# Three turning slots instead of six in the second pass of a channel-attention kernel

## The chip, the cores and the metric

The kernel runs on one core of a Trainium2 chip. The metric is the device time of one execution in microseconds (us). Each kernel is executed several times; the median is given with the lowest and the highest. One more execution is taken under the hardware profiler, and every row of a profile in this document comes from such an execution.

## The reference

The input x has 384 x 384 pixels of 384 channels in bfloat16. The reference takes the mean and the maximum of each channel over all pixels, sends both through the same two small matrices, adds the results, and scales every pixel of x by the sigmoid of the sum:

```python
gap = jnp.mean(xf, 1)
gmp = jnp.amax(xf, 1)
h_a = relu(gap @ w1); h_m = relu(gmp @ w1)     # written with a comparison and a cast
scale = _sigmoid(h_a @ w2 + h_m @ w2)
return x * scale[:, None, None, :]
```

So all of x has to be seen before the first output can be written. The input is 113.25 MB and so is the output. What doesn't fit on the chip between the two passes has to be read a second time.

## The kernel before

**Rows and blocks.** The pixels are counted in rows of 128 pixels, one pixel for each partition; there are 1152 such rows. A block of n rows is one transfer of 128 partitions with n x 768 bytes each; 44 rows are 4224 KB. On the chip there are six slots of 44 rows (`SLOTS`, L17, L118), a buffer `held` of 21 rows, a buffer `acc` of 11 rows for the running maximum, 16 rows kept in PSUM (`kept_ps`) and 2 more in a PSUM bank (`kept_b`).

**First pass (L179 to L207).** SP issues the reads (L184) into the slots in turn. For each block TensorE adds up the channels and VectorE folds the block into `acc` (L200). The last six blocks of 44 rows, the list `stay` (L84), are left in the six slots. `held`, `kept_ps` and `kept_b` hold the first rows of x until the end, and the 11 rows of `acc` are read again when the maximum is done (L228, L235). After that come the small matrices and the sigmoid, whose result stands in `scale_bc` (L241).

**Second pass (L244 to L311).** `put` (L255) multiplies a block by the scale on VectorE, in place (L246), and issues its store from ACT (L264). `get` (L268) reads one of the 20 blocks that are not on the chip, 18 of 44 rows and two of 23 (`AGAIN`, L34), into a slot, issued from SP (L273). The list `order` holds the blocks in the order of their stores. It begins with the six blocks that stayed. After two blocks have been put, the first two slots are read into; after every further block, the slot that has just been put is read into (`read_into`, L281), and the new block is added to the end of `order`. So the six slots turn over in a ring: each read waits until the store of the block six places earlier has landed. The first three blocks are multiplied and stored in small pieces (`FIRST_STORES`, L36), the first read comes in five pieces and the others in one (`FIRST_READS`, L38). When the ring has run out, `held` is multiplied and stored (L304, L305), then the 16 and 2 rows from PSUM, which are multiplied into the slot of the sixth last block, `order[-NS]` (L306 to L311).

**What sets the order.** On SP the instructions of the second pass run in the order in which the program writes them (L292). On the other engines a planner of the framework chooses an order; it may move an instruction forward where it reckons that the engine would otherwise wait. Each engine then runs its own instructions strictly in the planned order, and semaphores set by the framework make an instruction wait for its data or for its buffer.

Of the kernel before, what the change touches and what calls it, by code (L numbers as in the profile page):

```python
# [36 lines left out]

FIRST_READS = ((8, 8, 8, 10, 10), (44,))  # L38
LEAD = 2

ACC_STORES_AT = 3
SUM_TAIL = 4
# [4 lines left out]
def kernel(  # L47
# [15 lines left out]
    NS = len(SLOTS)  # L63
# [5 lines left out]
    def rows_of(ap, first, n):  # L69

        return ap[first * P:(first + n) * P, :].rearrange("(p n) c -> p n c", n=n)
# [12 lines left out]
    stay = []  # L84
# [159 lines left out]
    def multiply(dst, src):  # L244
        n = dst.shape[1]
        nc.vector.tensor_tensor(  # L246
            out=dst, in0=src, in1=scale_bc.unsqueeze(1).to_broadcast([P, n, C]), op=ALU.mult
        )

    def put_acc():  # L250
        for lo, hi in acc_pieces:
            multiply(acc[:, lo:hi, :], acc[:, lo:hi, :])
            nc.scalar.dma_start(out=acc_rows(orr, lo, hi), in_=acc[:, lo:hi, :])

    def put(block, pieces, acc_at=None):  # L255

        first, n, s = block
        j = 0
        for i, m in enumerate(pieces):
            if i == acc_at:  # L260
                put_acc()
            rows = slots[s][:, j:j + m, :]
            multiply(rows, rows)
            nc.scalar.dma_start(out=rows_of(orr, first, n)[:, j:j + m, :], in_=rows)  # L264
            j += m
        assert j == n
# [7 lines left out]
        assert j == 0  # L274


    order = list(stay)
    again.sort(key=lambda b: -b[1])
    stores, reads = list(FIRST_STORES), list(FIRST_READS)

    def read_into(s):  # L281
        fits = [b for b in again if b[1] <= SLOTS[s]]
        if fits:
            b = fits[0]
            again.remove(b)
            b = (*b, s)
            get(b, reads.pop(0) if reads else (b[1],))
            order.append(b)
# [5 lines left out]
    while k < len(order):  # L294
        put(order[k], stores.pop(0) if stores else (order[k][1],), None if k else ACC_STORES_AT)
        k += 1
        if k == LEAD:
            for j in range(k):
                read_into(order[j][2])
        elif k > LEAD:  # L300
            read_into(order[k - 1][2])
    in_order.close()
    assert not again
    multiply(held, held)  # L304
    nc.scalar.dma_start(out=rows_of(orr, held_at, HELD_ROWS), in_=held)  # L305
    s = order[-NS][2]  # L306
    n = PSUM_ROWS + BANK_ROWS
    multiply(slots[s][:, 0:PSUM_ROWS, :], kept_ps)
    nc.scalar.dma_start(out=rows_of(orr, 0, PSUM_ROWS), in_=slots[s][:, 0:PSUM_ROWS, :])
# [30 lines left out]
```

## Time and profile before

| | |
|---|---|
| median of 3 runs | 737.6 us (736.33 to 738.21) |
| profiled execution | 737.92 us |
| its span, first to last instruction | 736.1 us |
| bytes read, written | 196.85 MB, 113.25 MB |
| mean rate over the span | 421 GB/s |
| VectorE busy | 490.2 us, 67% of the span |
| TensorE matmul busy | 128.1 us, 17% of the span |
| 44-row reads of the second pass, issue to landing | 27.7 us median |
| 44-row stores, issue to landing | 79.7 us median |

A line of instructions gives the source line, the engine, the operation, what is written and read, and how often; the numbers behind it are busy time, the mean duration, and the idle time of the engine just before, with what ended it. The two hardware queues are q1 (issued from SP) and q10 (issued from ACT). The first pass ends and the second begins at about 276 us: the first multiply by the scale starts at 275.82. The last read lands at 689.88, and from then on only stores run.

### The profile page before, as it was taken

The numbers are of one execution on the slowest core, as the hardware profiler recorded it, in microseconds if no ns is written. First come the engines' busy times: TensorE is split into PE (matmuls) and PEld (weight loads), VectorE is DVE, ScalarE is ACT, GpSimd is POOL, SyncE is SP. The second block draws the span as 40 slices with busy tenths as digits, with TensorE's granted clock in tenths as the row PEclk, the third lists the DMA queues.
The fourth block names the chain that finished last, engine by engine and source line by source line (L and its number), as shares of the span: only waits on it lengthen the run. The fifth ranks groups of instructions, "written<-read, shape, count | busy, mean of one in ns | idle before, by whom it ended". The sixth has DMA issues, their size and how long they took to land.

```text
span 736.1 us, 2598 instructions
## 1 busy us (share of the span) xinstructions
PE 128.1 (17%) x969; PEld 41.1 (6%) x969; DVE 490.2 (67%) x286; ACT 3.3 (0%) x9; POOL 0.7 (0%) x6
## 2 busy tenths in 40 slices
PE   3334454454544550000000000000000000000000
PEld 0111111111111120000000000000000000000000
DVE  6789999999999989999444464444444444445400
ACT  0000000000000000000000000000000000000000
POOL 0000000000000000000000000000000000000000
PEclk9856667655556555555555555555555555555555
DMA  9999999999999979999999999999999999999998
GB/s 382 438 431 435 423 433 423 431 426 431 423 427 418 417 277 370 415 423 438 425 435 439 432 428 435 437 433 428 435 437 433 428 435 437 433 424 436 436 428 346
DMA packets 18956, 310.26 MB, mean 421 GB/s; under 512 B 2464, under 2 KB 3072, under 8 KB 8320
## 3 DMA queue, kind: packets, MB, share of 16 engines
q1 hardware_dynamic: 12464, 196.86, 63.0%
q10 hardware_dynamic: 6480, 113.25, 36.1%
q8 instruction: 7, 0.11, 0.1%
q14 instruction: 5, 0.04, 0.0%
HBM read 196.85 MB, written 113.25 MB: 421 GB/s over the span
## 4 chain that ended last, share of the span: by engine, by line
another core or an unknown queue 39%; DMA 39%; DVE 13%; DVEq 1%; SPq 1%; issue 1%; PE 0%; ACT 0%; ACTq 0%
DMA x<-in_x_dram 32%; DVE acc L200 10%; DMA out_dram<-x 7%; DVE x L246 2%; DVEq L335 1%; SPq L273 1%; SPq L184 0%; DVE acc L223 0%; DVE acc L246 0%; PE bank_a L240 0%; ACT scale_bc L241 0%; DVE small L234 0%; PE bank_a L233 0%; PE bank_a L238 0%
## 5 line engine op out<-in xcount | busy, mean ns | idle before, releaser
L246 DVE TENSOR_TENSOR x<-x,scale_bc 128x16896 bf16<-128x16896 bf16 (+11 forms) x40 | 224.9, 5665 | 188.6 <-DMA x<-in_x_dram 187.4
L200 DVE TENSOR_TENSOR acc<-acc,x 128x2304 bf16<-128x2304 bf16 (+5 forms) x221 | 241.4, 1167 | 12.6 <-DMA x<-in_x_dram 12.3
L157 PE MATMUL bank_a<-x,small 128*1 128x512 bf16 (+3 forms) x894 | 120.9, 571 | 140.4 <-DMA x<-in_x_dram 140.4
L157 PEld LDWEIGHTS <-small 128*1 128x1 bf16 x912 | 37.1, 110 | 229.2 <-issue 226.5
L193 DVE COPY acc<-x 128x4224 bf16<-128x4224 bf16 x1 | 1.3, 1260 | 5.2 <-DMA x<-in_x_dram 5.2
L200 DVE TENSOR_TENSOR acc<-acc,held 128x2304 bf16<-128x2304 bf16 (+2 forms) x4 | 4.6, 1201 | 0.0
L246 DVE TENSOR_TENSOR held<-held,scale_bc 128x8064 bf16<-128x8064 bf16 x1 | 4.4, 4351 | 0.0
L205 DVE COPY kept_ps<-x 128x3072 uint32<-128x3072 uint32 x1 | 3.4, 3355 | 0.0
L246 DVE TENSOR_TENSOR x<-kept_ps,scale_bc 128x6144 bf16<-128x6144 bf16 x1 | 3.4, 3350 | 0.0
L157 PE MATMUL bank_a<-held,small 128*1 128x512 bf16 (+1 forms) x18 | 2.4, 570 | 3.2 <-DMA held<-in_x_dram 3.2
L223 DVE TENSOR_TENSOR acc<-acc 128x384 bf16<-128x384 bf16 (+2 forms) x4 | 2.6, 658 | 0.1
L246 DVE TENSOR_TENSOR acc<-acc,scale_bc 128x1920 bf16<-128x1920 bf16 (+1 forms) x2 | 2.4, 1252 | 0.0
L168 ACT COPY w_sb<-bank_a 65x128 f32<-65x128 f32 x2 | 0.5, 262 | 265.2 <-PE bank_a L157 264.7
L174 PEld LDWEIGHTS <-x 128*128 128x128 bf16 x39 | 1.3, 109 | 0.0
L113 ACT ACT_TABLE_LOAD x1 | 1.3, 1283 | 0.7 <-PEq L324 0.7
L169 PE MATMUL bank_b<-small,w_sb 65*128 65x3 f32 x4 | 1.2, 365 | 0.4 <-ACT w_sb L168 0.4
L174 PE MATMUL bank_b<-small,x 128*128 128x1 bf16 x39 | 1.2, 165 | 0.0
L169 PE MATMUL bank_b<-small,scale_bc 65*128 65x3 f32 x4 | 1.1, 353 | 0.0
L169 PEld LDWEIGHTS bank_b<-small,w_sb 65*128 65x128 f32 x4 | 1.0, 313 | 0.9 <-ACT w_sb L168 0.9
L169 PEld LDWEIGHTS bank_b<-small,scale_bc 65*128 65x128 f32 x4 | 1.1, 323 | 0.0
L234 DVE TENSOR_REDUCE small<-bank_a 128x2 bf16<-128x256 bf16 x1 | 0.4, 427 | 0.6 <-PE bank_b L233 0.6
L233 PE MATMUL bank_a<-ident_bf,acc 128*128 128x128 bf16 x2 | 0.4, 301 | 1.9 <-DVE acc L223 1.9
(27 smaller groups left out, 7.5 us busy)
## 6 DMA issues: line engine op xcount, KB each, us to landing
out_dram<-x ACTq DMA_DIRECT2D x21, 4224.0 KB, 79.7
x<-in_x_dram SPq DMA_DIRECT2D x20, 4224.0 KB, 27.7
x<-in_x_dram SPq DMA_DIRECT2D x4, 4128.0 KB, 51.6
x<-in_x_dram SPq DMA_DIRECT2D x2, 4032.0 KB, 50.0
x<-in_x_dram SPq DMA_DIRECT2D x2, 3456.0 KB, 44.1
x<-in_x_dram SPq DMA_DIRECT2D x3, 2208.0 KB, 23.0
x<-in_x_dram SPq DMA_DIRECT2D x2, 2784.0 KB, 38.1
x<-in_x_dram SPq DMA_DIRECT2D x2, 2592.0 KB, 35.5
```

The costliest lines, as they stand in the source:

```text
L113: nc.scalar.activation(out=scale_bc[0:1, 0:1], in_=pick[0:1, 0:1], func=ACT.Sigmoid)
L157: nc.tensor.matmul(sum_ps[q * QP:q * QP + 1, 0:g * P], lhsT=ones_bf[:, 0:1], rhs=rows[:, k:k + g, q * P:(q + 1) * P], start=(done + k == 0 ...
L168: nc.scalar.copy(out=s_sb[r % 2], in_=sum_ps[:, r * P:(r + 1) * P])
L169: nc.tensor.matmul(gsum_ps, lhsT=s_sb[r % 2], rhs=pick, start=(r == 0), stop=False)
L174: nc.tensor.matmul(gsum_ps[:, q:q + 1], lhsT=rows[:, k, q * P:(q + 1) * P], rhs=ones_bf, start=False, stop=(last and k == n - 1 and q == C ...
L193: nc.vector.tensor_copy(out=acc, in_=rows[:, 0:A, :])
L200: nc.vector.tensor_tensor(out=acc[:, c:e, :], in0=acc[:, c:e, :], in1=rows[:, j:j + e - c, :], op=ALU.max)
L205: nc.vector.tensor_copy(out=kept_ps.bitcast(U32), in_=rows.bitcast(U32))
L223: nc.vector.tensor_tensor(out=acc[:, 0:h, :], in0=acc[:, 0:h, :], in1=acc[:, n - h:n, :], op=ALU.max)
L246: nc.vector.tensor_tensor(out=dst, in0=src, in1=scale_bc.unsqueeze(1).to_broadcast([P, n, C]), op=ALU.mult)
L273: nc.sync.dma_start(out=slots[s][:, j:j + m, :], in_=rows_of(xr, first, n)[:, j:j + m, :])
L335: with _tile.TileContext(nc) as tc:
```

## The change

Only the first three blocks of `stay` begin the ring. The other three, `resting`, keep their rows in their slots while the ring of three slots takes all 20 reads, and they are put whole, one after the other, when the loop has ended, before `held`. A read now goes into the slot of the block three places earlier. The rows kept in PSUM are multiplied into the slot of the third last block of the ring. The numbers of reads, multiplies, stores and bytes stay the same; the three resting blocks were also before multiplied and stored in one piece each.

```diff
+TURNING = 3
...
-    order = list(stay)
+    order, resting = list(stay[:TURNING]), list(stay[TURNING:])
...
     in_order.close()
     assert not again
+    for block in resting:
+        put(block, (block[1],))
     multiply(held, held)
     nc.scalar.dma_start(out=rows_of(orr, held_at, HELD_ROWS), in_=held)
-    s = order[-NS][2]
+    s = order[-TURNING][2]
```

## The prediction

> **What bounds the kernel now.** I read the page's slices and queues first, then stretches of the second pass, then who waits, then VectorE's order and the landing times. Busy tenths per fortieth of the span (18.4 us), and the two queues (q1 carries the reads that SP issues, q10 the stores that ACT issues):
>
> ```profile
> span 736.1 us, 2598 instructions
> DVE  6789999999999989999444464444444444445400
> DMA  9999999999999979999999999999999999999998
> GB/s 382 438 431 435 423 433 423 431 426 431 423 427 418 417 277 370 415 423 438 425 435 439 432 428 435 437 433 428 435 437 433 428 435 437 433 424 436 436 428 346
> q1 hardware_dynamic: 12464, 196.86, 63.0%
> q10 hardware_dynamic: 6480, 113.25, 36.1%
> ```
>
> The 16 DMA engines are busy 9 tenths or more nearly everywhere and take 99.1% of the span in these two queues; VectorE is below half in the second pass. Transfers bound the kernel, and the change moves no byte more or less. So the question is only whether some stretch of the second pass stops being full. Stretches of that pass (busy us of each engine with its count, granted clock, DMA share, GB/s last):
>
> ```profile
> 276.00:292.00 16.00, 0.00 (x0) 0.00 (x0) 16.00 (x14) 0.00 (x0) 0.00 (x0) 0.50 0.96 381
> 292.00:312.00 20.00, 0.00 (x0) 0.00 (x0) 20.00 (x7) 0.00 (x0) 0.00 (x0) 0.50 1.01 400
> 400.00:420.00 20.00, 0.00 (x0) 0.00 (x0) 8.97 (x2) 0.00 (x0) 0.00 (x0) 0.50 1.00 433
> 690.00:710.00 20.00, 0.00 (x0) 0.00 (x0) 8.45 (x3) 0.00 (x0) 0.00 (x0) 0.50 1.00 433
> 730.00:736.00 6.00, 0.00 (x0) 0.00 (x0) 0.00 (x0) 0.00 (x0) 0.00 (x0) 0.50 0.47 197
> ```
>
> Reads and stores mixed (400 to 420) and stores alone (690 to 710, after the last read landed at 689.88) move the same 433 GB/s at share 1.00. Only the opening, with its small pieces, and the last 6 us are below that. The waits of the second pass, of VectorE and of SP's queue (us in total, times, longest), and the landing times of the 44-row transfers between 360 and 640:
>
> ```profile
> DVE x L246 <- DMA x<-in_x_dram: 187.4, 18, 11.0
> SPq L273 <- DMA out_dram<-x: 376.2, 20, 23.7
> x<-in_x_dram SPq DMA_DIRECT2D x14, 4224.0 KB, 27.7
> out_dram<-x ACTq DMA_DIRECT2D x14, 4224.0 KB, 79.7
> ```
>
> A read waits for the store that empties its slot. A store takes 79.7 us, four times its share of the queue: four stores stand in line. VectorE's order in the middle (start, us, then the idle time before it):
>
> ```profile
> 399.85 8.96 DVE L246 TENSOR_TENSOR x<-x,scale_bc 128x16896 bf16<-128x16896 bf16 x1 [10.98 <-DMA x<-in_x_dram]
> 419.84 8.96 DVE L246 TENSOR_TENSOR x<-x,scale_bc 128x16896 bf16<-128x16896 bf16 x1 [11.03 <-DMA x<-in_x_dram]
> 428.71 4.35 DVE L246 TENSOR_TENSOR held<-held,scale_bc 128x8064 bf16<-128x8064 bf16 x1
> 439.79 8.96 DVE L246 TENSOR_TENSOR x<-x,scale_bc 128x16896 bf16<-128x16896 bf16 x1 [6.73 <-DMA x<-in_x_dram]
> ```
>
> One block (read, multiply, store) every 19.96 us, of which VectorE works 8.96. And the planner moves work: held is multiplied at 428.71, though its line stands behind the loop. Its store is issued at 695.13, in program order.
>
> **The change, part by part.** The same 20 reads, 26 slot multiplies and stores remain. A 44-row block is 4.325 MB: 10.0 us at 433 GB/s alone, 20.0 us at half of that. What changes is order.
>
> *Opening, until 311 us.* The first three blocks keep their pieces, and so do the first two reads. Cost 0: the rows are those above. VectorE ends the third block at 305.7; before, the fourth to sixth followed at once (three times 8.95).
>
> *Without those three stores in line.* Their place in q10 must be taken by stores of read blocks. The first read block lands at 316.18 (the chain of work; the other landings here are from the issues of single stretches), is multiplied by 325.2 and stored from then; the third block's last store (issued 306.99, landing after 28.3 us, so 335.3) still fills q10 meanwhile. The second read lands at 331.5 (issued 311.25, 20.2 us). From 335.4 the third read shares with the first read block's store. In program order q10 never empties: cost 0.
>
> *Steady turning with three slots.* SP's order puts nothing ahead of the next read but its own slot's store. A round of three blocks takes 3 x 19.96 = 59.9 us of DMA time. One slot's own chain is: SP's issue 0.3, first byte at most 1.7 (the shortest transfer of the pass, 96 KB, landed 1.7 after issue), read 20.0, multiply 8.96, store 20.0 = 51.0 us. The 8.9 us left over is time in which a finished block stands in q10 behind its predecessor, so q10 is never empty, and whenever q1 waits for its next read, q10 has both shares. Cost 0. ACT's issue, which in the trace of before waits at 351.69 and 372.27 for a store four earlier to land, has at most three in flight and stops waiting; worth 0, since the line was full anyway. If the 8.9 us were not there, see the short ring below.
>
> *The end.* Three resting multiplies (3 x 8.95) and stores (3 x 10.0) now lie behind the last read block. Let T be the landing that lets the last 23-row read start. That read (2.26 MB) and the store ahead of it (4.325 MB) take 15.2 us; the other 23-row store 5.2, to T+20.4. The last read lands by T+12.1, is multiplied (4.76) by T+16.9 and stored from T+20.4 to T+25.6. The first resting multiply ends at T+25.8 and its bytes flow by T+27.5: a hole of at most 1.9 us, if the planner leaves the program's order. After it VectorE makes a block in 8.95 and q10 needs 10.0, so no further hole. Held and kept pieces follow as before; kept waits for the slot of the third last ring block, long stored. The last 6 us at 197 GB/s end on the same two-row store: 0.
>
> *If the planner moves the resting multiplies forward*, as it did with held, the hole at the end is gone, and one can open where they stand. Nearest rows: all three and held (4.35) straight after the third block would end VectorE's run at 336.8, the first read block's store could start at 345.7, and q10 is empty from 335.3. The third read, issued at 335.4, runs alone until about 347: idle DMA is the first 1.7 us at most, plus 0.3. Put one by one in the gaps of 11.0, they cost 0 (8.95 fits). If their stores move forward too, they fill q10 as before: 0.
>
> *Sum.* Profiled execution: 737.92 for a span of 736.1; it stands 0.3 above the median of 737.6. The change adds 0 + 0 + 0 and between 0 and 2.0 for one hole, at the end or in the middle, not both. Below nothing: a gain is bounded by what is not full. The opening's 276 to 312 and the last 6 us lie 1.9 + 1.5 + 3.3 us above what 433 GB/s would need and are not touched, so I give at most -1. I take +0.6, nearer the low end, since only two of the orders considered open a hole: 737.6 + 0.6 = 738.2.
>
> **A rule that speaks against it.** The row: at share 1.00 and 19.96 us a block there is no recurring gap in the DMA. The Trainium skill, Perfetto Trace Analysis, section Optimization Strategy, says that a gap repeating on the engine that should be saturated can mean too few buffers; halving the turning buffers invites just that. By that rule a repeating hole would appear at each of 20 reads; by the row's spare 8.9 us none does. The skill's DMA: Bandwidth & Descriptors, section Anatomy of one DMA, fits about 2.0 us fixed per transfer (on another issue path than this one); exposed at 20 reads that would be an estimated 40 us, 778. No run here shows it exposed, and the stores in line cover it in my reckoning.
>
> **Rivals.** *The short ring becomes the bound* (slower). Place: SP's read waits at L273. For it: a read took 27.7 us before, and if a store took as long, the chain would be 27.7 + 8.96 + 27.7 + 0.3 = 64.7, 4.8 over 59.9, and with 20/3 rounds +32 us: 770. It decides once read plus store exceed 50.6 us with nothing in line ahead. Against: 7.7 of the 27.7 is standing behind the previous read (issued each 19.96), which a ring of three doesn't have.
>
> *VectorE holds the ring up* (slower). The planner puts 3 x 8.95 + 4.35 = 31.2 us of resting work in one lump before a ring multiply in the steady part. Cover: its 11.0 idle, 8.9 of waiting in line and 10.0 of a read running alone, 29.9; beyond it both queues are dry, 1.3 + 1.7 = 3.0 us: 740.6, more where such a lump stops the ring twice. It decides from a lump of about 30. For it: held was moved. Against: the idle times are 11.0, so lumps may well be split.
>
> *Faster.* Fewer transfers in flight could run nearer to the best slices of the first pass (438 GB/s): 1.2% of some 400 us, -4.6: 733. Against: mixed and lone stores both stand at 433 with share 1.00.
>
> *No change in effect*: stores and multiplies are both moved forward and the order is nearly that of before; 737.6, inside my forecast.
>
> **How the numbers follow.** A measurement of this kernel can tell about 0.3%, 2.2 us (735.4 to 739.8). Forecast, full throughout with at most one hole, "no change in effect" included: 0.64. VectorE lump: 0.15 (739.9 to 745). Short ring: 0.12 (741 to 770). Faster: 0.09 (731 to 735.3). The range leaves out the upper two thirds of the short ring (0.08) and most of the faster case (0.07): 735.0 to 745.0. Same 0.64, slower 0.27, faster 0.09.
>
> **What would show it.** Right: stretches of 20 us between 340 and 660 at 432 or more; 44-row stores landing in 25 to 40 us instead of 79.7; reads near 20 to 23; VectorE still idle some 11 before each ring multiply; the last read landing some 52 us before the end (25.6 - 12.1 + 30 + held and kept 8.9) where it was 45. Wrong: share below 0.98 in the steady stretches (short ring), a single dip beside a row of resting multiplies (lump), a rate above 436 (faster). The forecast fails if a lone queue with one transfer in flight cannot fill 16 engines: before had deeper lines wherever one queue was alone.

## The result and the profile after

| | median us | lowest to highest | runs |
|---|---|---|---|
| before | 737.05 | 736.33 to 738.21 | 5 |
| after | 740.95 | 740.37 to 742.09 | 5 |

The ratio is 1.0051, with a 95% interval of 1.0036 to 1.0065. The kernel became 3.9 us slower, half a percent. The time lies inside the stated range, but the likeliest case, full throughout with at most one hole and no change to be told (735.4 to 739.8), is not what happened. On another chip the change was measured once more at 1.0036 (1.0023 to 1.0049).

The page of the changed kernel, the lines that answer to those of before:

```profile
span 739.3 us, 2595 instructions
DVE  6789999999999989959564441444444444444440
DMA  9999999999999979999999999999999999999988
GB/s 380 436 431 433 423 431 435 432 426 428 420 428 420 414 265 371 423 427 441 433 411 430 439 439 432 424 433 437 439 435 426 430 435 439 437 426 429 413 353 383
q1 hardware_dynamic: 12464, 196.86, 62.7%
q10 hardware_dynamic: 6480, 113.25, 36.1%
```

Bytes and packets are those of before. The low slices stand at the very end: 413, 353 and 383, where before had 436, 428 and 346. (The 411 in the 21st slice holds the stretch from 375 to 380, at 385 GB/s, but there the two queues' packets together still take 62.8% and 37.7% of the engines' time; in the second profile of the same kernel that stretch is at 433, so it is no mark of the change.) Stretches of the second pass, the steady part first (us of each engine, clock, DMA share, GB/s last):

```profile
400.00:420.00 20.00, 0.00 (x0) 0.00 (x0) 8.98 (x2) 0.00 (x0) 0.00 (x0) 0.50 1.00 433
560.00:580.00 20.00, 0.00 (x0) 0.00 (x0) 9.00 (x2) 0.00 (x0) 0.00 (x0) 0.50 1.00 433
680.00:690.00 10.00, 0.00 (x0) 0.00 (x0) 8.19 (x1) 0.00 (x0) 0.00 (x0) 0.50 0.96 408
690.00:700.00 10.00, 0.00 (x0) 0.00 (x0) 4.76 (x1) 0.00 (x0) 0.00 (x0) 0.50 1.06 434
700.00:710.00 10.00, 0.00 (x0) 0.00 (x0) 2.20 (x1) 0.00 (x0) 0.00 (x0) 0.50 0.95 391
710.00:720.00 10.00, 0.00 (x0) 0.00 (x0) 6.29 (x3) 0.00 (x0) 0.00 (x0) 0.50 0.69 293
```

The steady part is as full with three slots as it was with six: 433 GB/s at share 1.00. From 680 on there is a small dip and then a hole. Against 433 the four last stretches lack 25, -1, 42 and 140 GB/s for 10 us each, 4.8 us of transfer in all; before, the same four stretches (446, 433, 433, 410) lacked 0.2. The last landing is only 3.1 us later in these two executions (738.27 against 735.15), so about 1.5 us of that sum may be coarse counting rather than loss: a packet is counted at its start. Summed by the durations of the packets in the trace, the 16 engines stand idle for 0.4 us in all between 688 and 689.5 and for 2.8 us between 710.5 and 713.5 (in the second profile of the change 0.9 and 3.6 us); before, no stretch between 312 and 730 shows such an idle time. The heart of the hole:

```profile
710.50:713.50 3.00, 0.00 (x0) 0.00 (x0) 3.00 (x2) 0.00 (x0) 0.00 (x0) 0.50 0.18 77
```

Who issues what around the hole:

```profile
688.22 25.20 ACTq L265 DMA_DIRECT2D out_dram<-x  x4
688.75 0.33 SPq L274 DMA_DIRECT2D x<-in_x_dram  x1
690.77 4.76 DVE L247 TENSOR_TENSOR x<-x,scale_bc 128x8832 bf16<-128x8832 bf16 x1 [2.58 <-DMA x<-in_x_dram]
707.80 4.76 DVE L247 TENSOR_TENSOR x<-x,scale_bc 128x8832 bf16<-128x8832 bf16 x1 [12.28 <-DMA x<-in_x_dram]
712.47 3.35 DVE L247 TENSOR_TENSOR x<-kept_ps,scale_bc 128x6144 bf16<-128x6144 bf16 x1
713.45 0.95 ACTq L308 DMA_DIRECT2D out_dram<-held  x1
```

The last read is issued at 688.75 and lands at 707.7. VectorE needs until 712.5, and only then does ACT issue the last ring block's store (712.59), and behind it at once the stores of a resting block (712.97) and of held (713.45). The store ahead had moved its last bytes by 712 and landed at 712.25; the first bytes of the new stores move at 713.4. In between nothing is under way, although held and the resting block had been multiplied long before:

```profile
333.82 17.83 DVE L247 TENSOR_TENSOR x<-x,scale_bc 128x16896 bf16<-128x16896 bf16 x2 [8.42 <-DMA x<-in_x_dram]
359.94 17.83 DVE L247 TENSOR_TENSOR x<-x,scale_bc 128x16896 bf16<-128x16896 bf16 x2 [8.29 <-DMA x<-in_x_dram]
377.69 4.35 DVE L247 TENSOR_TENSOR held<-held,scale_bc 128x8064 bf16<-128x8064 bf16 x1
```

Each of the two runs of 17.83 us is a ring block and a resting block behind it; the first resting block is multiplied even earlier, at 305.8. The planner moved all three multiplies into VectorE's first gaps. It moved two of the three stores along (ACT issues them at 314.76 and 369.31) but left the third behind the last ring block, in the program's place. So only one block is in fact "stored near the end", and ACT, which issues in order, can't send it while it waits for the last multiply.

Why the last read took 18.9 us where 12.1 had been reckoned, the queues between 691 and 704 show (packets, MB, share of 16 engines):

```profile
q10 hardware_dynamic: 105, 3.31, 65.1%
q1 hardware_dynamic: 103, 1.82, 32.6%
```

Both queues send nearly the same number of packets, not the same number of bytes. A packet of q1 has 1.82 MB / 103 = 17.7 KB, the 23 rows of one partition; those of q10 are mostly 33.8 KB, the 44 rows of one. The 23-row read beside the 44-row store therefore gets about a third of the rate (1.82 of 5.13 MB), and the two transfers of 128 partitions, issued at 688.75 and 688.22, land at 707.7 and 706.4, though one is nearly twice as long. This is not all of the delay: the packets of the read run from 692.8 to 706.7. That is 13.9 us where half the rate would give 10.4; the first of them starts 4.1 us after issue, where 1.7 had been taken (the read ahead lands only at 690.7), and the landing comes 1.0 us after the last.

### The profile page after: what moved, and what is told of

Its sections match the earlier page's. It is cut to its first block, busy times and chain, and to the rows that moved or that the text cites. A ratio compares the mean times of both kernels' runs of the same rounds, so it can differ in the third digit from the quotient of the medians.

```text
span 739.3 us, 2595 instructions
## 1 busy us (share of the span) xinstructions
PE 130.0 (18%) x969; PEld 41.6 (6%) x969; DVE 490.4 (66%) x286; ACT 3.3 (0%) x9; POOL 0.7 (0%) x6
## 4 chain that ended last, share of the span: by engine, by line
DMA 77%; DVE 17%; DVEq 1%; issue 1%; SPq 0%; PE 0%; ACT 0%; ACTq 0%
DMA x<-in_x_dram 53%; DMA out_dram<-x 24%; DVE x L247 10%; DVE acc L201 7%; DVEq L338 1%; DVE acc L224 0%; SPq L185 0%; DVE acc L247 0%; PE bank_a L241 0%; ACT scale_bc L242 0%; DVE small L235 0%; PE bank_a L234 0%; PE bank_a L239 0%; DVEq L247 0%; DVE small L240 0%
## 5 line engine op out<-in xcount | busy, mean ns | idle before, releaser
L158 PE MATMUL bank_a<-x,small 128*1 128x512 bf16 (+3 forms) x894 | 122.8, 579 | 138.5 <-DMA x<-in_x_dram 138.5
## 6 DMA issues: line engine op xcount, KB each, us to landing
out_dram<-x ACTq DMA_DIRECT2D x21, 4224.0 KB, 23.6
x<-in_x_dram SPq DMA_DIRECT2D x20, 4224.0 KB, 27.2
x<-in_x_dram SPq DMA_DIRECT2D x3, 2208.0 KB, 18.9
```

The source lines that it names most:

```text
L158: nc.tensor.matmul(sum_ps[q * QP:q * QP + 1, 0:g * P], lhsT=ones_bf[:, 0:1], rhs=rows[:, k:k + g, q * P:(q + 1) * P], start=(done + k == 0 ...
```

## Experiments

Three theories were to be told apart. **The empty line**: the whole loss is at the end, where q10 runs dry because ready stores stand behind the last ring block's store. **The short ring**: three slots lose a little at each turn. **Late stores**: storing blocks late costs by itself. All ratios are to the kernel before on the same chip.

**The resting blocks before the last two ring blocks.** In program order; the planner still moves two of them forward, and the third now stands in ACT's order ahead of the two 23-row stores.

```diff
     while k < len(order):
+        if not again and k == len(order) - 2:
+            for block in resting:
+                put(block, (block[1],))
         put(order[k], ...)
...
-    for block in resting:
-        put(block, (block[1],))
```

> The resting blocks are put before the last two ring blocks instead of after them; ring, reads and bytes as in the change. Theory of the empty line (all of the added 3.9 us is a hole at the end, where ACT waits with ready stores behind the last block's store): the last resting store of 10 us stands in line while the last read is awaited, no hole, 737.0 (736.3 to 737.8). Rival, ring of three too short (a little lost at each turn): the ring is the same, 741. Rival, stores kept for late cost by themselves: 741, since they are as late but for one block.

Measured: 738.07, ratio 1.0015 (1.0006 to 1.0024). Most of the loss went with the place of one store in ACT's order, so neither rival holds for the whole. But 1 us stayed, and 738.07 is above the 737.8 that the theory allowed. Its profile (of an execution that at 740.92 was the slowest of its twelve) shows where:

```profile
680.00:690.00 10.00, 0.00 (x0) 0.00 (x0) 8.96 (x1) 0.00 (x0) 0.00 (x0) 0.50 0.86 370
710.00:720.00 10.00, 0.00 (x0) 0.00 (x0) 7.69 (x2) 0.00 (x0) 0.00 (x0) 0.50 1.01 434
```

The hole at 710 is closed (434 for 293), the dip at 680 to 690 is not: by the durations of the packets the engines idle for 1.3 us there. Whether the usual execution, near 738, has as large a dip is not shown.

**The resting blocks straight after the first three**, as before the change, but their slots not used again. Only the ring is shortened.

```diff
+        if k == TURNING:
+            for block in resting:
+                put(block, (block[1],))
...
-    for block in resting:
-        put(block, (block[1],))
```

> The resting blocks are put straight after the first three blocks, as before the change, but their slots are not read into again: only the ring is shortened. Empty line: at the end ACT still has nothing in line but the last two ring blocks, so the hole stays, 741 (740 to 742.5), perhaps longer as one ready store less follows. Rival, ring too short: 741 too, with the loss spread over the turns instead of in the last 40 us. Rival, late stores: 737.

Measured: 740.17, ratio 1.0042 (1.0030 to 1.0054), with stretches of 364 and 316 GB/s from 710 to 730 and 434 from 640 to 680. The loss stays with no block stored late: the theory of late stores falls. Short ring and empty line both allow this time; the place of the low stretches speaks for the latter.

**Four slots turn.**

```diff
-TURNING = 3
+TURNING = 4
```

> Four slots turn, two rest. Empty line: one more 44-row store (10 us) stands in line when the last read is issued, more than the hole of about 4 us, so the hole is gone whole: 737.0 to 737.8. Rival, ring too short with a loss by the number of slots: a part of the 3.9 us stays, 738 to 740. Rival, late stores: two thirds of 3.9 us, 739.7.

Measured: 736.94, ratio 0.9994 (0.9981 to 1.0006). One more store in line and the loss is gone whole, not by a third. The last ring block's multiply of this kernel, and the stores behind it:

```profile
688.27 4.76 DVE L247 TENSOR_TENSOR x<-x,scale_bc 128x8832 bf16<-128x8832 bf16 x1 [10.42 <-DMA x<-in_x_dram]
693.06 1.35 ACTq L265 DMA_DIRECT2D out_dram<-x  x3
694.45 0.46 ACTq L308 DMA_DIRECT2D out_dram<-held  x1
```

It, too, leaves two resting stores and held behind the last block. But the last block is through at 693, when the store ahead of it still needs until 699.7.

**The store of the last 44-row ring block in two halves**, all else as in the change.

```diff
+        halved = not again and k == len(order) - 3
+        pieces = (22, 22) if halved else (order[k][1],)
-        put(order[k], stores.pop(0) if stores else (order[k][1],), ...)
+        put(order[k], stores.pop(0) if stores else pieces, ...)
```

> The change, with the store of the last 44-row ring block in two pieces of 22 rows. Packets of one partition's run alternate between the two queues, so a 23-row read beside a 44-row store ends only with that store (18.9 us after issue, where 12.1 was reckoned); beside 22-row stores it should get half and land about 6 us earlier, 12 to 13 us after issue. Then the last block's store is ready before the one ahead of it is through: hole mostly gone, 737.0 to 738.0. Rival, the 23-row read is slow for a reason of its own: still 18 to 19 us after issue and 740 to 741. The first half can be stored some 4.5 us earlier, which by itself is worth at most the 1 us dip before that store.

Measured: 736.92, ratio 0.9997 (0.9989 to 1.0006). The last read, issued at 686.77, took 14.1 us instead of 18.9, a little above the expected 12 to 13 and not the 18 to 19 of a read that is slow by itself. Behind it the queues between 688 and 700, where both send packets of some 17 KB:

```profile
x<-in_x_dram SPq DMA_DIRECT2D x1, 2208.0 KB, 14.1
q10 hardware_dynamic: 170, 2.60, 50.5%
q1 hardware_dynamic: 164, 2.54, 49.4%
```

The packets of the read take 9.7 us (690.1 to 699.9) instead of 13.9: that is 4.2 of the 4.8 us gained.

```profile
680.00:690.00 10.00, 0.00 (x0) 0.00 (x0) 6.28 (x2) 0.00 (x0) 0.00 (x0) 0.50 1.00 428
700.00:710.00 10.00, 0.00 (x0) 0.00 (x0) 5.63 (x3) 0.00 (x0) 0.00 (x0) 0.50 1.01 434
```

Both holes are closed, the early dip as well, since the first half is stored 4.5 us sooner. So this run shows that the length of the neighbour's packets sets the read's rate, but not how much of the kernel's gain is due to that and how much to the earlier first half.

**Two slots turn**, to measure the chain of a slot itself.

```diff
-TURNING = 3
+TURNING = 2
```

> Two slots turn, four rest. By the chain of one slot as predicted (0.3 + 1.7 + 20.0 + 8.96 + 20.0 = 51.0 us) against 2 x 19.96 = 39.9 us of transfers, the ring is the bound and each round of two blocks loses up to 11.1 us: for about 9 rounds not filled by a resting block some +100, 840. As reads and stores then often run alone and so faster than at half rate, the chain shrinks: between 44 and 48 us a round, +35 to +75, 772 to 812, is what I expect. Rival, two slots would do as well as three (slack much larger than the 8.9 us reckoned): 737 to 742.

Measured in two executions: 797.07, ratio 1.0807 (1.0783 to 1.0831). The 44-row transfers between 500 and 740, and two stretches:

```profile
x<-in_x_dram SPq DMA_DIRECT2D x10, 4224.0 KB, 19.1
out_dram<-x ACTq DMA_DIRECT2D x10, 4224.0 KB, 20.1
```

```profile
520.00:540.00 20.00, 0.00 (x0) 0.00 (x0) 8.96 (x1) 0.00 (x0) 0.00 (x0) 0.50 0.85 329
540.00:560.00 20.00, 0.00 (x0) 0.00 (x0) 6.49 (x1) 0.00 (x0) 0.00 (x0) 0.50 0.85 355
```

Here the ring is the bound: the five stretches of 20 us from 500 to 600 are at shares of 0.85 to 0.98. The chain is 19.1 + 9.0 + 20.1 = 48.2 us, a little above the expected 44 to 48 and below the 51.0 of the prediction. Two slots need it to be under 39.9, three under 59.9. This is what a short ring looks like, and the change shows nothing of it.

**The resting blocks before the last two ring blocks, and held before the last.**

```diff
+        if not again and k == len(order) - 1:
+            multiply(held, held)
+            nc.scalar.dma_start(out=rows_of(orr, held_at, HELD_ROWS), in_=held)
```

> As with the resting blocks before the last two ring blocks, and held before the last ring block. Empty line: both stores stand in line while the last read is awaited; no hole, 736.5 to 737.5, the same as before the change within 0.15%; nothing is left to gain but the opening and the last 6 us, so not below 736. Rival, ring too short: 740 to 741.

Measured: 738.27, ratio 1.0013 (1.0000 to 1.0027). This is above the expected 736.5 to 737.5, and held in front of the last block adds nothing to the move of the resting blocks. But its profile, of an execution at 738.39, shows no hole:

```profile
680.00:690.00 10.00, 0.00 (x0) 0.00 (x0) 7.43 (x2) 0.00 (x0) 0.00 (x0) 0.50 0.97 417
710.00:720.00 10.00, 0.00 (x0) 0.00 (x0) 6.29 (x3) 0.00 (x0) 0.00 (x0) 0.50 0.96 411
```

Before has 410 in the second of these stretches without an idle engine, and by the durations of the packets the engines are full here from 680 to 720. So with the same transfers in the same order up to 690 the dip is there in one execution, that of the first experiment, and absent in another; what makes the 0.13% here, whose interval begins at no loss, stays open.

**The resting blocks before the last three ring blocks**: `len(order) - 3` for `len(order) - 2` in the first experiment's edit. Beside it the change itself, on the same chip.

> The resting blocks one ring block earlier still, before the last three. Reading so far: there are two holes, both of the empty line. The shorter 23-row reads let the store beside them end early, so the last 44-row ring block's store also comes a little late (the stretch 680 to 690 of the change at 408 GB/s, some 0.6 to 1.3 us); moving the resting blocks before the last two ring blocks closed only the second hole and left 0.15%. With the resting store ahead of the last 44-row block both are covered: 736.5 to 737.5, no stretch of 10 us between 640 and 710 under 425 GB/s. Rival, what is left after the second hole is a loss of the three-slot ring itself: still 0.1 to 0.2% above before, 738.

> The change itself, on the same chip as the kernel with the resting blocks before the last three, as the measure of what moving them recovers. Both theories: 740 to 742, with the stretch from 710 to 720 near 293 GB/s again.

Measured: 736.93, ratio 0.9994 (0.9985 to 1.0003), against 739.92, ratio 1.0036 (1.0023 to 1.0049), for the change. With one more ring block behind the resting store, nothing is left to lose, with the same ring of three (the change itself came out just under the 740 to 742 that were expected):

```profile
670.00:680.00 10.00, 0.00 (x0) 0.00 (x0) 1.83 (x1) 0.00 (x0) 0.00 (x0) 0.50 0.96 413
680.00:690.00 10.00, 0.00 (x0) 0.00 (x0) 7.12 (x1) 0.00 (x0) 0.00 (x0) 0.50 1.02 440
690.00:700.00 10.00, 0.00 (x0) 0.00 (x0) 4.76 (x1) 0.00 (x0) 0.00 (x0) 0.50 0.98 422
700.00:710.00 10.00, 0.00 (x0) 0.00 (x0) 1.29 (x1) 0.00 (x0) 0.00 (x0) 0.50 1.00 431
710.00:720.00 10.00, 0.00 (x0) 0.00 (x0) 7.29 (x3) 0.00 (x0) 0.00 (x0) 0.50 1.02 438
```

Two stretches, at 413 and 422, are under the 425 that was named. By the durations of the packets the engines are full in both, so this is the coarse counting: the mark of 425 was too fine for 10 us. In the change's own second profile, of an execution at 742.68, the slowest of its seven, the stretch from 710 to 720 stood at 277.

None of the versions beats the kernel before beyond its interval; the three at 736.9 are equal to it.

## Why the prediction was right or wrong

**The bound, right.** Transfers bound both kernels, and the time moved only where a stretch was not full.

**Opening, right.** Cost 0: the stretches there are as full as before within 2 GB/s, and the first read block lands at 316.37 where 316.18 was taken over.

**Steady turning, right in the sum, wrong in part of the picture.** No loss, as said. But it was said that the spare time of a round would be spent by finished blocks waiting in q10, with reads of 20 to 23 us and stores of 25 to 40. In the profile after it is the other way round (44-row transfers from 460 to 640):

```profile
out_dram<-x ACTq DMA_DIRECT2D x9, 4224.0 KB, 23.6
x<-in_x_dram SPq DMA_DIRECT2D x9, 4224.0 KB, 27.2
```

Reads wait 7.2 us behind the read before (27.2 less the period of 20.0), stores only 3.6. With 9.0 of multiplying these make 59.8, the round of 59.9. The spare time exists, the two-slot kernel puts it at 59.9 - 48.2 = 11.7, but here most of it lies in front of the reads. How it divides differs between executions; in the second profile of the change, in the same stretch, the stores have the larger part:

```profile
out_dram<-x ACTq DMA_DIRECT2D x9, 4224.0 KB, 25.9
x<-in_x_dram SPq DMA_DIRECT2D x9, 4224.0 KB, 24.9
```

The dip at 680 to 690 comes where the first 23-row read replaces a longer one: the store beside it landed after 20.5 us (at 688.70) instead of 23.6, and the next block's store was issued only at 688.22 and moved its first bytes at 689.1. A small spare in front of the stores does not explain the size of the dip, since the second profile, with 5.9 us to spare, lost more there (0.9 us for 0.4). What sets its size stays open.

**The end, wrong: this is the step that failed.** It put the last read's landing at T+12.1, by giving the read half the rate. It landed at T+19.0 (T is 688.70): halves are halves of packets and not of bytes, which made 3.5 us of the difference, and the rest is its late first packet and its landing. Its multiply then ended at T+23.9 instead of T+16.9, and the store ahead, reckoned to T+20.4, was through at T+23.6: the 3.5 us by which the last block's store should have been early had become 0.3 us too late, plus the time until the first bytes flow. The rows that tell it were in the trace of before: between 315 and 325 a 44-row read (q1) ran at over three times the rate of the store's short pieces, and the last 23-row read, issued at 668.66, itself took 21.2 us.

```profile
q1 hardware_dynamic: 108, 3.29, 76.4%
q10 hardware_dynamic: 118, 1.03, 26.1%
668.66 21.23 DMA x<-in_x_dram
```

**"If the planner moves the resting multiplies forward, the hole at the end is gone", wrong.** The multiplies moved, the third store did not. The prediction's own rows had shown this pattern for held, multiplied at 428.71 and issued at 695.13, and had drawn no conclusion from it for the end. With the ready stores ahead of the last three blocks', in the last experiment, the time was that of before, though the last read took 20.9 us there: a late read costs nothing here as long as ready stores stand in line. The sign that was named for the end fails with this step too: the last read landed 30.6 us before the last store's landing, not 52, since two of the three resting stores had gone ahead.

**The sum.** Between 0 and 2.0 for one hole; there were a dip and a hole, 3.9 us together, about twice the most that was allowed. That the time still lies in the stated range is luck: the range went up to 745 for the VectorE lump, which did not happen.

**The rivals.** VectorE holding the ring up had the nearest time (740.6), but not the mechanism: the planner put the resting multiplies one at a time, the last with held behind it, into gaps, and no stretch in their neighbourhood ran dry: in the change's second profile 360 to 400 is at 433 throughout. The short ring is real at two slots and absent at three. Of the faster case nothing is seen: no stretch of 20 us from 340 to 660 ran above 434.

**The skill's rules.** A gap that repeats where buffers are too few, as the Trainium skill (Perfetto Trace Analysis, Optimization Strategy) has it, appears at two slots (shares of 0.85 to 0.98) and not at three (1.00); the change's hole does not repeat, it comes once. A fixed cost of about 2.0 us for each transfer, which the skill's DMA: Bandwidth & Descriptors, section Anatomy of one DMA, fits for another issue path, is nowhere exposed in the steady part at 433 GB/s. The same page's section Queues, rings and completion order says that an engine goes round its queues packet by packet. The 103 and 105 packets of the two queues agree; the prediction had not made use of that.

## What to carry to other kernels

Halving the buffers of a ring that is bound by transfers was free here for the whole pass and still cost at its end, where the depth of the line was what hid the last read and its multiply: look at what is ready when the last read is under way, and put its stores ahead of the last block's in the issuing engine's own order. A planner that moves a compute step forward does not have to move the store behind it, so check both orders. And reckon the shares of two queues by packets, not by bytes: here a 23-row read beside a 44-row store ended only when the store did.

## What was not expected of the hardware

Two queues under load sent nearly equal numbers of packets, with packets as long as the contiguous run of one partition: 103 of 17.7 KB against 105 of 31.5 KB on average in 13 us. The share of a 23-row read beside a 44-row store was therefore 1.82 of 5.13 MB, 35%, and with the store's run length halved the read took 14.1 us instead of 18.9.
